# A fused attention and ResMLP kernel: the first pair's lam products and the beta1 of batches 2 and 3 on VectorE, and the second-matmul operand of product 3 cast by every pair

## The chip, the cores and the metric

The kernel runs on one core of a Trainium2 chip. The metric is the device time of one execution in microseconds (us), and the time of a version is the median over its runs. Engines are named as in the profile: PE is TensorE (PEld its weight loads), DVE is VectorE, ACT is ScalarE, POOL is GpSimd, SP is SyncE, which here only issues transfers.

## The reference, cut to what matters

Grouped-query attention (16 query heads, 4 key heads, head size 64, 8 batches of 384 positions) is followed by one ResMLP block on the 1024 channels:

```python
x   = attention(q, k, v)                      # 8 batches of 384 x 1024
a1  = alpha1 * x + beta1
tok = einsum('ts,bsd->btd', w_tok, a1)        # mixes the 384 positions
u   = x + lam * tok
a2  = alpha2 * u + beta2
ch  = maximum(a2 @ w_ch1, 0) @ w_ch2          # 1024 -> 4096 -> 1024
out = u + lam * ch
```

All inputs and the output are float32; the kernel's matmuls take bf16.

## The kernel before

**Pairs and products.** The eight batches are taken in four pairs (pair 0 holds batches 0 and 1, and so on). For a pair, each of the two channel matmuls is done as seven products of half-size blocks in place of eight, from sums and differences of the blocks of both operands. Products are numbered 1 to 7. A pair has a first product stage (`w_ch1`) and a second (`w_ch2`). In the trace the first stage of pair 0 is line 681, its second stage line 752; for pairs 1 to 3 these are lines 831 and 897.

**What runs beside them.** While the second stage of pair i runs, the attention and the token mixing of the two batches of pair i+1 are interleaved with it on every engine: `side(b)` makes the steps of batch b, and a plan (`put(pair, stage, step, function)`) says at which step of the stage each is issued. Each engine works through its instructions in the program's order. For each of the eight column blocks p of a batch, `av_piece` computes attention times v (L295), the reciprocal (L300), x (L303) and alpha1*lam*x; `tok` mixes positions (PE L324), adds (L331) and multiplies by alpha2 (L334); `turn` transposes the result on PE (L398).

**beta1.** For batches 0 to 3 (`fold`) beta1 is not added on DVE. Its effect on tok is an outer product of the row sums of w_tok (R) and of lam*beta1 (H), which PE adds by one more matmul per 128x128 output block (L328); DVE then needs one instruction per block (L309). For batches 4 to 7 DVE does a product (L312) and a sum with h1 = lam*beta1 (L313). H and R lie in the memory of h1, so h1 is loaded (`rows4_on`: two POOL memsets and two small SP transfers; `to_all` L1037; `scale_beta` L1040) only in the first stage of pair 1.

**lam times ch.** Each finished 128x512 piece of ch is multiplied by lam (`scaled`, L790) and added to the output in HBM by an accumulating POOL transfer (`store`, L442). Twelve pieces belong to pair 0; nine of these multiplications are issued in its second stage and three in the first stage of pair 1. For pair 0 they are done on POOL, for later pairs on DVE.

**Operands of the second stage.** Each product has a 2048x512 operand from `w_ch2`, handled as four chunks of 128x2048 bf16 (512 KB). Product 3's operand is the quadrant "22" itself; others are quadrants or differences. In pair 0 the quadrants are read from HBM by POOL transfers that cast float32 to bf16 (L491), DVE forms the differences (`sum_w2`, L499), and `keep_w2` (L494, on SP's queue) writes all 28 chunks to the scratch tensor `w2s` in HBM. Pairs 1 to 3 read them back in the order of `PLACE2` (products 1, 2, 6, 5, 3, 7, 4) by `fetch` (L528, SP's queue) into slots of `w1` or `pad` as PE frees them; product 3 has chunks 16 to 19.

**From pair 0 to pair 1.** At the end of pair 0's second stage DVE forms sums of the turned a2 blocks (`sums_a`, L448 to L450) and of the chunks of w_ch1 (`sum_w1`, L510 and L515). Chunks of w_ch1 are loaded by `load_w1` (POOL, L183) into freed slots; `order1` takes chunk g and chunk g+8 in turn, so the four that open pair 1 are 0, 8, 1, 9. The sum for the next step, `sum_w1(1, 5)`, needs chunk 9. In DVE's order it stands ahead of the sum that makes block 6 of the left operand (L850), which product 3 of the first step needs: that is the tenth of the fourteen matmul groups of a step (`SEQ1`).

Of the kernel before, what the change touches and what calls it, by code (L numbers as in the profile page):

```python
# [13 lines left out]
def kernel(  # L14
# [21 lines left out]
    nc = tc.nc  # L36
# [4 lines left out]
    MUL = mybir.AluOpType.mult  # L41
# [43 lines left out]
    g1, h1, al2, lam_t = (vecs[:, i] for i in range(4))  # L85
# [10 lines left out]
    turn, a2_turn = [0], [0]  # L96
# [21 lines left out]
    SLOTS = 7 * NH // 4  # L118
    w2s = [tc.dram_tile([P, NDT * CW * P], bf, name=f"w2s{i}") for i in range(SLOTS)]
    PLACE2 = {o: i for i, o in enumerate((1, 2, 6, 5, 3, 7, 4))}  # L120

    def by_tok(ap):
        return ap.rearrange("(p st) d -> p st d", st=NST)
# [90 lines left out]
    def side(b):  # L214
        vb = vt[b % 2]
        ess, avs, a1s, a2s, xr = {}, {}, {}, {}, {}
        first, fold = b < 2, b < 4
        kT_, qT_ = kTs.get(b, kT), qTs.get(b, qT)

        def x_of(p):  # L220
# [170 lines left out]
        def by_pe(p):  # L391
            return b in (0, 3) or b % 2 and p >= NP - (4 if first else 3)
# [14 lines left out]
        def put(k, *m):  # L407
            at.setdefault(k, []).append(m)
# [3 lines left out]
        for p in range(NP):  # L412
            put((4, 10, 14, 18, 24, 29, 33, 35)[p], av, p)
            put((8, 15, 17, 22, 27, 32, 36, 38 if b % 2 else 39)[p], tok_flip, p)
            if by_pe(p):
                put(((13, 20, 22, 28, 34, 37, 40, 42) if b == 3 else (0, 0, 0, 0, 0, 36, 39, 41))[p], turn, p)
        return at

    def loads(b):
# [21 lines left out]
    def store(b, ms, dw, o):  # L441
        nc.gpsimd.dma_start(out=by_tok(out[b])[:, ms, dw * 512:(dw + 1) * 512], in_=o, accum_op=ADD)  # L442
# [19 lines left out]
    def spare(i):  # L462
        at = 24 * S + i % 3 * 1024
        return hTf[:, at:at + 1024]

    raw = {}
# [4 lines left out]
    def w2_block(name, c):  # L471
        kh, dw = int(name[0]) - 1, int(name[1]) - 1
        return w2src[:, kh * NH + 4 * c:kh * NH + 4 * c + 4, dw * 512:(dw + 1) * 512]

    def stored(c):
        return w2s[4 * PLACE2[2] + c]

# [13 lines left out]
            nc.gpsimd.dma_start(out=at.rearrange("p (a c) -> p a c", a=4), in_=w2_block(name, c))  # L491

    def keep_w2(o, c):
        nc.sync.dma_start(out=w2s[4 * PLACE2[o] + c], in_=raw[{1: "11", 3: "22", 5: "12", 6: "12", 7: "11", 4: "again"}[o], c][1])  # L494

    def sum_w2(o, c):
        at = lambda name: raw[name, c][1]
        to, x, y = {5: ("12", "12", "11"), 6: ("12", "22", "12"), 7: ("11", "12", "11"), 4: ("again", "again", "12")}[o]
        tt(out=at(to), in0=at(x), in1=at(y), op=SUB)  # L499
        keep_w2(o, c)  # L500
# [17 lines left out]
    w2_slots, w2_at = {}, {}  # L518
# [3 lines left out]
    def place(slot):  # L522
        return ring[:, slot] if slot < RING else pad[:, (slot - RING) * 2048:(slot - RING + 1) * 2048]

    def fetch(i, n):
        w2_slots[i, n] = slot = (pad_free if n in PADDED else w1_free).pop(0)
        w2_at[i, n] = place(slot)
        nc.sync.dma_start(out=w2_at[i, n], in_=w2s[n])  # L528

    def free(slot):  # L530
        (w1_free if slot < RING else pad_free).append(slot)
# [35 lines left out]
    def free_blocks(side, gp):  # L567
        for kind in (side + "1", side + "2"):
            if (kind, gp) in block_slot:
                free(block_slot.pop((kind, gp)))  # L570
# [7 lines left out]
    for i in range(1, NB):  # L578
        heads = [(load_w1, c) for c in order1[:4]] if i + 1 < NB else []
        queue += [(load_w1, c) for c in order1[4:]] + [(fetch, i, n) for n in range(SLOTS - 2)] + heads[:2]  # L580
        queue += [(fetch, i, n) for n in (SLOTS - 2, SLOTS - 1)] + heads[2:]
# [190 lines left out]
    def pair(i):  # L772
        b0 = 2 * i
        lead = i == 0
# [12 lines left out]

        def scaled(o, b, ms, dw, t):
            if o != 2 or not last:
                (nc.gpsimd if lead else nc.vector).tensor_tensor(out=t, in0=t, in1=lam_t[:, dw * 512:(dw + 1) * 512], op=MUL)  # L790
            store(b, ms, dw, t)

        def flush(n=9):
# [18 lines left out]
        if lead:  # L812
            yield from first_product(flush)
            share_banks("sc0", "acc", "sc1", "sc2")
            yield from second_product(pairs["acc"], later, flush, scaled)
            return

        for g in range(NH // 2):
            X, Y, snap = {}, {}, {}
            for k, (o, e) in enumerate(SEQ1):  # L820
                t = 2 * g + e
# [53 lines left out]
        where = {2: (0, 0), 3: (0, 1), 7: (1, 1), 4: (1, 0)}  # L875
        for k, o in enumerate(PLACE2):
            whole = not last and o != 4
            tail = last and o == 4
            for h in range(1 if whole else 2):
                for ms in range(NST - (tail and not h)):  # L880
# [37 lines left out]
                    if (whole or h == 1) and not (last and o == 4):  # L918
                        if o in (1, 6, 5):
                            q = ((1, 6, 5).index(o) * NST + ms) * 512  # L920
                            snap[o, ms] = snaps[:, q:q + 512]
                        else:
                            bb, dw = where[o]
                            t = snap[1, ms] if o == 7 else spare(ms).bitcast(f32)
                        for c0, c1, x in X[ms]:
                            if o == 1:
                                nc.scalar.copy(out=snap[o, ms], in_=x)
                            elif o in (6, 5):
                                tt(out=snap[o, ms], in0=x, in1=snap[1 if last or o == 6 else 6, ms], op=ADD)
                            elif o == 2 and last:  # L930
                                tt(out=t, in0=x, in1=lam_t[:, :512], op=MUL)
                            else:
                                base = {2: 1, 3: 1 if last else 5, 7: 5, 4: 6}[o]
                                tt(out=t[:, c0:c1], in0=x, in1=snap[base, ms][:, c0:c1], op=ADD)
                            if o == 7 and not last:
                                tt(out=snap[6, ms], in0=x, in1=snap[6, ms], op=ADD)
                        if o not in (1, 6, 5):
                            later.append((scaled, o, b0 + bb, ms, dw, t))
# [8 lines left out]
    with tc.manual_schedule(engines=order):  # L947
# [123 lines left out]
        def put(ps, phase, at, *m):  # L1071
            plan.setdefault((ps, phase, at), []).append(m)
# [17 lines left out]
        put(0, 0, 8, rows4_on, (3, 0), (3, 1))  # L1090
        put(0, 0, 30, to_all, 3, 0, 0)
        put(0, 0, 34, to_all, 3, 1, 1)
        put(1, 0, 20, rows4_on, (1, 0), (1, 1))
        put(1, 0, 54, to_all, 1, 0, 0)
        put(1, 0, 68, to_all, 1, 1, 1)
        put(1, 0, 62, scale_beta, 0)
        put(1, 0, 76, scale_beta, 1)
        for c in range(4):
            put(0, 0, (50, 72, 74, 44)[c], load_w2, "11", c)
            put(0, 0, (6, 14, 42, 46)[c], cast_w2, "21", c)  # L1100
            put(0, 1, (41, 43, 45, 47)[c], keep_w2, 1, c)
            put(0, 1, 38 + 2 * c, keep_w2, 3, c)
            put(0, 1, (9, 10, 13, 15)[c], sum_w2, 5, c)
            put(0, 1, (20, 21, 25, 26)[c], sums_first_hid, 2, c)
            put(0, 1, (28, 30, 31, 34)[c], sums_first_hid, 4, c)
            put(0, 1, (37, 40, 41, 43)[c], sum_w2, 6, c)
            put(0, 1, (44, 45, 49, 50)[c], sums_first_hid, 3, c)
            put(0, 1, (51, 54, 57, 58)[c], sum_w2, 7, c)
            put(0, 1, (61, 64, 68, 71)[c], last_w2, c)
        for u, o in ((77, 5), (79, 7), (81, 6)):  # L1110
            put(0, 1, u, sum_w1, 0, o)
        for ps in range(NB - 1):
            c = 2 * ps + 2
            for i in range(9):
                put(ps, 0, (4, 8, 12, 16, 20, 24, 54, 58, 62)[i] if ps == 0 else 4 + 7 * i, load_next, c, 1)
                put(ps, 0, 70 + 3 * i if ps == 0 else 91 + 2 * i, load_next, c + 1, 1)
            put_flips(ps, 0, c, (44, 46, 50, 54, 58) if ps == 0 else range(76, 86, 2))
            put_all(ps, 1, side(c))
            for u, f, h in zip((8, 14, 14, 27, 32, 33) if ps == 0 else (10, 17, 18, 28, 33, 33),
                               (flip_q, flip_k, flip_q, flip_q, flip_k, flip_q), (0, 0, 2, 4, 2, 6)):  # L1120
                put(ps, 1, u, f, c + 1, h, 2)
            put_all(ps, 1, side(c + 1), lambda u: u + 38)
            for j, u in ((0, 77), (2, 80), (3, 83)) if ps == 0 else ((0, 76), (2, 79), (3, 81)):
                put(ps, 1, u, sums_a, j, 1 if j else 2)

        def steps(ps):
            done = [0, 0]
            for second in pair(ps):
                for f, *a in plan.pop((ps, second, done[second]), []):
                    f(*a)  # L1130
                done[second] += 1
                yield
            for key in [k for k in plan if k[0] == ps]:
                for f, *a in plan.pop(key):
                    f(*a)

        first = steps(0)
# [76 lines left out]
```

## Time and profile before

| what | value |
|---|---|
| median of 3 runs | 732.88 us (731.51 to 733.32) |
| the profiled execution's own time | 731.92 us |
| its span in the trace | 729.9 us |
| TensorE clock granted | 1.0 |
| PE busy | 717.4 us |
| DVE busy | 543.9 us |
| POOL busy | 199.2 us |
| DMA queue of POOL (software) | 64.47 MB, 65.4% of 16 engines' span |
| DMA queue of SP (hardware) | 87.42 MB, 42.8% |

The span runs from the first to the last recorded instruction of one execution; 2.0 us of its time lie outside. A busy share is time in which an engine has an instruction in it. "Idle before" gives the idle time of an engine ahead of an instruction and what ended it. The share of a DMA queue is the time of its packets, waiting included, so two queues can add up to more than 100%.

### The profile page before, as it was taken

To read this page: it belongs to the slowest core of one execution; us is meant where nothing else is said; L and a number is where in the kernel's file an instruction comes from. 1 tells how busy PE (TensorE), PEld (TensorE's weight loads), DVE (VectorE), ACT (ScalarE), POOL (GpSimd) and SP (SyncE) were. 2 spreads that over 40 slices of the span, in tenths; PEclk is the share of its full clock that TensorE was granted. 3 is DMA by queue.
4 is the path that set the end of the run, shared out by engine and by line. 5 is a ranking of instruction groups with operands and counts; after the bars stand their busy time and mean duration, and the time that the engine had idled before them with its cause. 6 is when DMAs were issued, how large, how long until landed. Compare 5 with 4: busy or idle time off the path is not lost.

```text
span 729.9 us, 14511 instructions
## 1 busy us (share of the span) xinstructions
PE 717.4 (98%) x5716; PEld 408.7 (56%) x5716; DVE 543.9 (75%) x1009; ACT 373.8 (51%) x566; POOL 199.2 (27%) x242
## 2 busy tenths in 40 slices
PE   8899999999999999999999999999999999999998
PEld 4665555555555666555555566655555566654444
DVE  7888876577888988649678888748868988763354
ACT  7877666544563666643433466663333366650000
POOL 8844233221046551201022344200002222000011
PEclk9999999999999999999999999999999999999999
DMA  9999999999999999969989999998989999937965
GB/s 164 180 239 231 190 195 227 226 242 235 366 312 232 179 182 196 234 221 207 272 193 220 160 162 194 212 227 201 270 233 183 210 126 146 165 123 264 302 174 104
DMA packets 197616, 153.26 MB, mean 210 GB/s; under 512 B 90540, under 2 KB 175892, under 8 KB 197292
## 3 DMA queue, kind: packets, MB, share of 16 engines
q0 software_dynamic: 109872, 64.47, 65.4%
q1 hardware_dynamic: 86988, 87.42, 42.8%
q8 instruction: 44, 0.72, 0.4%
q10 hardware_dynamic: 688, 0.46, 0.2%
q14 instruction: 24, 0.20, 0.1%
HBM read 155.23 MB, written 39.85 MB: 267 GB/s over the span
## 4 chain that ended last, share of the span: by engine, by line
PE 90%; DVE 4%; POOL 2%; DMA 1%; issue 1%; ACT 1%; DVEq 0%; ACTq 0%; POOLq 0%
PE C L897 30%; PE X L831 17%; PE C L752 10%; PE Y L831 9%; PE Z L831 4%; PE sc L260 4%; PE X L681 4%; PE sc L295 3%; PE sc L324 3%; PE Y L681 3%; DMA ops<-obuf 1%; DVE pad L565 1%; PE Z L681 1%; PE tok L324 1%; POOL obuf L334 0%
## 5 line engine op out<-in xcount | busy, mean ns | idle before, releaser
L897 PE MATMUL C<-w,arena 128*128 128x512 bf16 (+2 forms) x744 | 168.3, 372 | 0.0
L269 ACT ACTIVATE es<-sc 128x1024 bf16<-128x1024 f32 x108 | 104.1, 1024 | 116.0 <-PE sc L260 107.6
L897 PEld LDWEIGHTS <-arena 128*128 128x128 bf16 x1040 | 94.8, 98 | 100.5 <-issue 5.1
L442 POOL DMA_DIRECT2D out_dram<-hT x45 | 40.0, 888 | 294.7 <-DVE hT L790 135.9
L836 ACT ACTIVATE hT<-X,bias 128x384 f32<-128x384 f32 x144 | 83.6, 582 | 60.0 <-PE X L831 55.2
L831 PEld LDWEIGHTS <-w 128*128 128x128 bf16 x768 | 75.1, 98 | 50.0
L831 PEld LDWEIGHTS <-pad 128*128 128x128 bf16 x576 | 56.4, 98 | 37.2
L183 POOL DMA_DIRECT2D w<-in_moe_w_ch_dram x48 | 45.4, 1002 | 105.6 <-PE X L831 36.5
L831 PE MATMUL X<-ops,w 128*128 128x384 bf16 x384 | 70.3, 326 | 0.0
L831 PE MATMUL X<-ops,pad 128*128 128x384 bf16 x384 | 70.3, 326 | 0.0
L897 PE MATMUL C<-pad,arena 128*128 128x512 bf16 (+2 forms) x296 | 70.2, 373 | 0.0
L324 PEld LDWEIGHTS <-wtokT 128*128 128x128 bf16 x576 | 39.0, 98 | 16.4 <-issue 3.4
L752 PEld LDWEIGHTS <-arena 128*128 128x128 bf16 x336 | 29.8, 98 | 30.0 <-issue 2.5
L331 DVE TENSOR_TENSOR xr<-sc,xr 128x384 f32<-128x384 f32 x48 | 26.5, 553 | 25.6 <-PE sc L324 14.3
L752 PE MATMUL C<-w,arena 128*128 128x512 bf16 x168 | 41.2, 379 | 0.0
L838 DVE TENSOR_TENSOR arena<-Y,hT 128x384 bf16<-128x384 f32 x48 | 26.5, 556 | 17.7 <-ACT hT L836 16.0
L295 PEld LDWEIGHTS <-es 128*128 128x128 bf16 x864 | 32.8, 97 | 11.3
L831 PE MATMUL Y<-ops,w 128*128 128x384 bf16 x192 | 39.1, 326 | 0.0
L831 PE MATMUL Z<-ops,w 128*128 128x384 bf16 x192 | 39.0, 326 | 0.0
L269 ACT ACTIVATE hT<-sc 128x1024 bf16<-128x1024 f32 x36 | 35.8, 1031 | 4.3 <-PE sc L260 4.0
L260 PE MATMUL sc<-qT,kT 64*128 64x384 bf16 (+2 forms) x504 | 37.2, 271 | 0.5 <-ACT hT L269 0.2
L842 ACT ACTIVATE arena<-X,bias 128x384 bf16<-128x384 f32 x48 | 27.9, 582 | 17.7 <-PE X L831 16.1
(190 smaller groups left out, 1175.1 us busy)
## 6 DMA issues: line engine op xcount, KB each, us to landing
w<-w2s SPq DMA_DIRECT2D x67, 512.0 KB, 5.1
w<-in_moe_w_ch_dram POOLq DMA_DIRECT2D x65, 512.0 KB, 9.8
pad<-w2s SPq DMA_DIRECT2D x25, 512.0 KB, 6.9
out_dram<-hT POOLq DMA_DIRECT2D x45, 256.0 KB, 7.1
out_dram<-xr SPq DMA_DIRECT2D x48, 192.0 KB, 5.3
q_raw<-in_q_dram POOLq DMA_DIRECT2D x28, 192.0 KB, 9.5
w2s<-w SPq DMA_DIRECT2D x10, 512.0 KB, 7.6
arena<-in_moe_w_ch_dram POOLq DMA_DIRECT2D x8, 512.0 KB, 15.9
```

The lines of the kernel that those rows point to most:

```text
L183: nc.gpsimd.dma_start(out=w1[:, w1_slots[c]], in_=w1src[:, :, c * CW * P:(c + 1) * CW * P])
L260: nc.tensor.matmul(out=sc[:, hh, k % 4:k % 4 + n], lhsT=kT_[r, 2 * p // G, BLK[hh][sk], :], rhs=qT_[r, p, st:st + n, :], start=True, stop= ...
L269: nc.scalar.activation(out=e, in_=sc, func=EXP, scale=scale_qk)
L295: nc.tensor.matmul(out=av[:, hh, sq, :], lhsT=ess[k // 4][:, m % 2, k % 4, :], rhs=vb[:, sk, hk, :], start=(sk == 0), stop=(sk == NST - 1))
L324: nc.tensor.matmul(out=ps[:, tt, :], lhsT=wtokT[:, st, tt * P:(tt + 1) * P], rhs=a1s[p][:, st, :], start=(st == 0), stop=(st == NST - 1 an ...
L442: nc.gpsimd.dma_start(out=by_tok(out[b])[:, ms, dw * 512:(dw + 1) * 512], in_=o, accum_op=ADD)
L681: nc.tensor.matmul(out=ps[:, :n], lhsT=tb[G, o][:, dt, e * P:(e + 1) * P], rhs=opb(FIRST1[o], n)[:, dt], start=(o in (1, 2, 7) and dt == 0 ...
L752: nc.tensor.matmul(out=x, lhsT=lead_hid[:, t, FIRST2[o], ms * P:(ms + 1) * P], rhs=rhs[:, t % 4 * 512:(t % 4 + 1) * 512], start=(o in (1, ...
L831: nc.tensor.matmul(out=ps, lhsT=tb[g, o][:, dt, e * P:(e + 1) * P], rhs=opb(LEFT1[o])[:, dt], start=(o in (1, 2, 7) and dt == 0), stop=(dt ...
L836: nc.scalar.activation(out=snap[o, e], in_=ps, func=IDENT, bias=hi if o == 5 else lo)
L842: nc.scalar.activation(out=hid[:, t, 4], in_=ps, func=RELU, bias=hi)
L897: nc.tensor.matmul(out=x, lhsT=hid[:, t, LEFT2[o], ms * P:(ms + 1) * P], rhs=rhs[:, t % 4 * 512 + c0:t % 4 * 512 + c1], start=((not last o ...
```

## The change

Three parts. `fold` now holds for batches 0 and 1 only, so batches 2 and 3 add beta1 on DVE; h1 is loaded in the first stage of pair 0 instead of that of pair 1. The lam multiplication of pair 0 is on DVE like that of the others. Chunks 16 to 19 are no longer written by `keep_w2`; `fetch` reads them from `w_ch2` in each of pairs 1 to 3 by a casting POOL transfer. One PE transpose of batch 3 (block 2) is placed a step later.

```diff
+    RAW2 = {PLACE2[3]: "22"}
-        first, fold = b < 2, b < 4
+        first = fold = b < 2
-                put(((13, 20, 22, 28, 34, 37, 40, 42) if b == 3 else (0, 0, 0, 0, 0, 36, 39, 41))[p], turn, p)
+                put(((13, 20, 23, 28, 34, 37, 40, 42) if b == 3 else (0, 0, 0, 0, 0, 36, 39, 41))[p], turn, p)
     def keep_w2(o, c):
-        nc.sync.dma_start(out=w2s[4 * PLACE2[o] + c], in_=raw[{1: "11", 3: "22", 5: "12", 6: "12", 7: "11", 4: "again"}[o], c][1])
+        nc.sync.dma_start(out=w2s[4 * PLACE2[o] + c], in_=raw[{1: "11", 5: "12", 6: "12", 7: "11", 4: "again"}[o], c][1])
     def fetch(i, n):
-        nc.sync.dma_start(out=w2_at[i, n], in_=w2s[n])
+        if n // 4 in RAW2:
+            nc.gpsimd.dma_start(out=w2_at[i, n].rearrange("p (a c) -> p a c", a=4), in_=w2_block(RAW2[n // 4], n % 4))
+        else:
+            nc.sync.dma_start(out=w2_at[i, n], in_=w2s[n])
         def scaled(o, b, ms, dw, t):
-                (nc.gpsimd if lead else nc.vector).tensor_tensor(out=t, in0=t, in1=lam_t[:, dw * 512:(dw + 1) * 512], op=MUL)
+                nc.vector.tensor_tensor(out=t, in0=t, in1=lam_t[:, dw * 512:(dw + 1) * 512], op=MUL)
-        put(1, 0, 20, rows4_on, (1, 0), (1, 1))
-        put(1, 0, 54, to_all, 1, 0, 0)
-        put(1, 0, 68, to_all, 1, 1, 1)
-        put(1, 0, 62, scale_beta, 0)
-        put(1, 0, 76, scale_beta, 1)
+        put(0, 0, 40, rows4_on, (1, 0), (1, 1))
+        for i in range(2):
+            put(0, 0, 54 + 10 * i, to_all, 1, i, i)
+            put(0, 0, 59 + 10 * i, scale_beta, i)
-            put(0, 1, 38 + 2 * c, keep_w2, 3, c)
```

## The prediction

> **What bounds the kernel now.** I read the page's engine shares first, then the busy time by stretches of 20 us, then the chain of waits from 215 us on, and last the groups of instructions and the timeline around the places that stand out.
>
> ```profile
> span 729.9 us, 14511 instructions
> PE 717.4 (98%) x5716; PEld 408.7 (56%) x5716; DVE 543.9 (75%) x1009; ACT 373.8 (51%) x566; POOL 199.2 (27%) x242
> ...
> 200.00:220.00 20.00, 19.41 (x194) 10.97 (x193) 16.81 (x24) 12.64 (x19) 8.04 (x8) 1.00 1.19 309
> 220.00:240.00 20.00, 18.81 (x141) 10.53 (x138) 16.51 (x28) 8.84 (x17) 10.48 (x11) 1.00 1.18 227
> 240.00:260.00 20.00, 20.00 (x125) 12.04 (x124) 19.15 (x31) 13.21 (x23) 12.06 (x14) 1.00 1.38 178
> ```
>
> The columns after the stretch are its length, then PE, PEld, DVE, ACT and POOL busy, the clock, the DMA share and GB/s. PE sets the end: from 240 to 720 us every stretch has it 20.00 of 20. Its idle 12.5 us (729.9 - 717.4) are the head (some 7 us to 120 us), the tail (3.6) and 1.8 in 200 to 240 us, the end of pair 0's second stage. So this change can gain in two ways, PE work removed and those 1.8 us; what it adds elsewhere costs only where it makes PE wait.
>
> ```profile
> 218.18 0.06 PE sc L328
> ...
> 220.87 2.02 DVE w L499
> ...
> 223.62 1.09 DVE a L309
> 224.71 0.04 issue
> 224.76 0.34 PE sc L324 x3
> ```
>
> This is the chain (start, length, what). A beta1 matmul holds it for 0.06 us, and at 224.76 PE waits for DVE's L309.
>
> ```profile
> L309 DVE TENSOR_TENSOR a<-xr,vecs 128x384 bf16<-128x384 f32 x16 | 11.8, 736 | 0.6
> L312 DVE TENSOR_TENSOR a1f<-xr,vecs 128x384 f32<-128x384 f32 x32 | 17.9, 558 | 1.1
> L313 DVE TENSOR_TENSOR a<-a1f,vecs 128x384 bf16<-128x384 f32 x32 | 17.8, 557 | 1.1
> L790 DVE TENSOR_TENSOR hT<-hT,vecs 128x512 f32<-128x512 f32 x30 | 20.6, 686 | 0.4
> L790 POOL TENSOR_TENSOR hT<-hT,vecs 128x512 f32<-128x512 f32 x12 | 18.6, 1552 | 17.6 <-ACT hT L764 17.6
> ...
> 225.19 1.56 POOL L790 TENSOR_TENSOR hT<-hT,vecs 128x512 f32<-128x512 f32 x1
> 225.44 1.74 DVE L309 TENSOR_TENSOR a<-xr,vecs 128x384 bf16<-128x384 f32 x1
> ```
>
> The same DVE product takes 0.56 us undisturbed (L312) and 1.74 beside a POOL product: the two block each other, and L309's mean of 736 ns is 16 x 0.18 = 2.9 us of such blocking.
>
> **The change part by part.** *PE work removed.* 16 blocks lose three L328 matmuls each, 48 in all. In the chain a mixing step takes 3 x (0.17 + 0.06) us with them and 0.50 without (batches 4 and 5), so 0.17 per block and 16 x 0.17 = 2.7 us. All of it lies where PE is the chain, between 138 and 228 us.
>
> *DVE in pair 0's second stage.* Added: 16 x 0.56 (a product becomes a product and a sum) = 8.9 us and nine lam products x 0.69 = 6.2 us. Returned: the blocking, 2.9 us on L309 and some 2.6 on others (L334 at 212.75 took 1.77 for 0.56, L499 at 220.87 2.02 for 1.22, L334 at 149.16 1.05 for 0.56). Net +9.6 us. Between 142 and 229 us DVE has about 14 us of idle time, most of it before 193. There the extra work is covered: at 156.5, 163, 169, 178.7 and 189 DVE waited 1.0 to 1.9 us for PE, more than the 0.6 to 1.2 that one block gains. Without that cover it would be up to 9.6 us. The cover ends at 212 us, so I walk the rest in the order of the new program.
>
> *The walk.* I use starts on DVE, one to the next, since instructions overlap by some 0.08 us: L303 and L312 0.59, L313, L309 and L334 0.47, L331 0.58, L300 0.22, lam 0.61, L499 1.14, L767 0.60. DVE waits last for ACT's copy of C that ended at 214.7; thirteen mixing steps lie ahead of it, so it comes 13 x 0.17 = 2.2 earlier, at 212.5. From there DVE has, without a pause, two L767 (1.2), three sets of L300, L303, product and sum (3 x 1.87 = 5.6), six lam products (3.7), two L499 (2.3), three pairs of L331 and L334 (3.2), one L515 (0.6) and the first three `sums_a` (1.5): 18.1 us, and the sixth lam product ends at 230.6. In the walk the wait of 0.95 us at 224.76 remains: the sum ends at 222.1 where PE is ready at 221.1. PE reaches the end of the stage at 231.7 instead of 234.54, 2.8 earlier.
>
> *What is late next.* DVE's `sums_a` end near 233.7 and PE wants block 0 at 233.0: some 0.4 us. More decides the load of chunk 9. On POOL's queue it stands behind the six stores, and each store now waits for DVE's lam product instead of POOL's own; so do the loads and k, q and v transfers behind it. Before, the last store was issued at 227.05 and chunk 9 at 232.10, when PE freed its slot:
>
> ```profile
> 232.10 0.92 POOL L183 DMA_DIRECT2D w<-in_moe_w_ch_dram  x1 [4.17 <-PE sc L398]
> ...
> 238.07 0.69 DVE L515 TENSOR_TENSOR pad<-w 128x1024 bf16<-128x1024 bf16 x1 [2.92 <-DMA w<-in_moe_w_ch_dram]
> ...
> 238.68 0.95 DVE L850 TENSOR_TENSOR ops<-ops 128x1536 bf16<-128x1536 bf16 x1
> ```
>
> DVE stood 2.92 us for that chunk, and L850, which PE's group at 240.39 needs, came right behind it: 0.76 us in hand. Now the sixth store is issued at 230.7 and chunk 9 at 231.6, only 0.5 earlier than before, while PE has come 2.8 earlier. With the 5.9 us to landing that it had, it lands at 237.6; POOL's software queue carries the late store ahead of it (the last six stores took 11.6 falling to 7.5 us to land, a queue working off a backlog), so I take 238.0, between that and a delay of one store's spacing (1.7 us). Then L515 (0.61) and L850 (0.95) end at 239.6, and PE's group starts there, not at 240.39: **0.8 us of the 2.7 are left**, the rest goes into a wait of about 1.5 us before that group and 0.4 before block 0.
>
> A fixed-cost rule speaks for more. The Trainium skill, page "DMA: Bandwidth & Descriptors", section "Anatomy of one DMA", gives a software transfer about 2.0 us plus its bytes at 436 GB/s; my estimate from it is 4.4 us for the 1 MB read here, and the sum would be that of the first rival. The trace has 5.6 to 13.7 us for these loads, and I go by the trace.
>
> *Pair 1's first stage.* Three lam products move to DVE (2.1 us), the h1 work leaves it (two L1037 of 0.72, two L1040 of 0.68: 2.8 us), and the blocking at 244.57 (L861 1.90 for 0.36) and 246.57 (L863 1.43 for 0.56) goes. DVE gains; nothing for PE, which has no wait there. *First stage of pair 0.* The same 2.8 us and two memsets (0.6 each, POOL idle) arrive; DVE waited 1.8 to 2.2 us for PE once in each group of 9.4 us there, which covers about 1.2 a group. Bounds 0 to 0.6 us, I take 0. The later transpose costs nothing: PE does it anyway.
>
> *Product 3's chunks.* Four writes of 512 KB leave SP's queue in the stretch where it is busiest (0.4 to 1.6 us of issue each). Twelve SP reads (landing 3.1 to 8.9 us) become POOL casts, issue 0.75 us each. In pair 1 SP issued chunks 16 to 19 at 339.5, 346.9, 350.0 and 353.3; PE uses them first at 365.2, 366.6, 367.4 and 369.1, so 16 to 26 us in hand. POOL is idle from 339.6 to 371.9, and the stores ahead of them in its order are out by 338.75. Such casts took 5.8 to 22.7 us, the long ones six in a row; these come 3 to 7 us apart, and I take 13: hidden. Pair 2 is the same to 1 us; in pair 3 the hand is 16 to 20 us. Bounds: 0, and 22.7 - 15.8 = 6.9 us for each of pairs 1 to 3.
>
> *Sum.* Span 729.9 - 2.7 + 1.9 = 729.1; the profiled execution 731.92 becomes 731.1. It lay 0.96 below the median of the runs, so against 732.88 the forecast is **732.1 us**.
>
> **Rivals.** *The full PE gain.* If chunk 9 lands by 236.4, L850 is in time and only 0.4 is lost: 732.88 - 2.4 = 730.5. For it: stores landed in 4.1 us at other places, SP's writes of product 3 no longer share the engines. Against: no load landed in under 5.6. *Slower: POOL's queue behind DVE.* If the late store and three loads run into a queue still full, chunk 9 takes what the loads at 251 to 272 us took (8.5 to 13.7 us, behind stores). With 10.6 us it lands at 242.2, L850 ends at 243.8, 3.4 after the group's old start: 736.3. It decides above a landing of 7.2 us, where the gain is gone. For it: the median of these loads, 9.4; against: that neither the loads of k, q and v nor spills crowd this moment. *Casts not hidden.* At the upper bound 3 x 6.9 = 21 us, 754; with a landing of 17.8 us, 2 each, 739. *DVE binds the whole second stage* or the change does less on PE than it says: the built programs show 48 matmuls and weight loads fewer, and DVE would need its 9.6 us uncovered: 732.9 - 2.7 + 5 = 735 at half.
>
> **How the numbers follow.** Forecast 0.45, full gain 0.22, POOL's queue 0.23, casts 0.06, DVE 0.04. A change under 0.3% (2.2 us) can't be told from none here. Faster beyond it is the full gain and the forecast's edge (0.24), slower most of the last three (0.30), the rest 0.46. The forecast's own range is 731.6 to 734.1 (landing 5.9 to 8.4); the whole range takes in the full gain and the queue's typical case: 729.9 to 736.6.
>
> **What would show it.** L328 with 48 matmuls fewer and L309 or its successors at 0.56 us; no POOL product at L790; the idle time of DVE's L515 before L850, and PE waiting for L850 in its first step of pair 1; chunk 9 issued right behind a store near 231.6. PE waits at line 897 in pairs 1 to 3 would prove the casts wrong; a stage boundary 2.8 us earlier with no wait behind it the first rival right.

## The result and the profile after

The changed kernel took 736.91 us (median of 20 runs), the kernel before 732.6 us beside it: a ratio of 1.0068 (95% interval 1.005 to 1.0086). That is 4.3 us slower; 732.1 was forecast, 0.8 us faster than the kernel before. The ratio leaves out the executions that were counted as slow, the medians hold all. The profiled execution took 736.13 us with a span of 734.4, 4.5 more than the span before. Line numbers have moved by one to four: L790 is now L794, L831 L835, L850 L854, L515 L516, L183 L184, L442 L443.

First the page's head (shares, the PE row and the clock row in 40 slices of 18 us) and the busy time by stretches (length, PE, PEld, DVE, ACT, POOL, clock, DMA share, GB/s), of the changed kernel:

```profile
span 734.4 us, 14411 instructions
PE 718.7 (98%) x5668; PEld 406.4 (55%) x5668; DVE 551.1 (75%) x1037; ACT 373.6 (51%) x566; POOL 190.4 (26%) x242
...
PE   8899999999998899999999999999999999999998
...
PEclk9999999999999899999999999999999999999999
```

```profile
200.00:220.00 20.00, 19.76 (x205) 10.94 (x204) 18.93 (x31) 14.66 (x21) 3.53 (x4) 1.00 1.09 288
220.00:240.00 20.00, 16.68 (x107) 8.63 (x103) 13.51 (x28) 6.98 (x13) 6.84 (x8) 1.00 1.06 185
240.00:260.00 20.00, 18.34 (x97) 10.37 (x98) 15.42 (x28) 10.36 (x17) 7.49 (x9) 0.83 1.10 148
```

PE has 48 matmuls fewer and yet is busy 1.3 us longer; in 240 to 260 us it got through 97 recorded matmuls (125 before) at a granted clock of 0.83 (1.00 before). Two things are new: a gap around 240 us, and slow products behind it.

The groups that the change was to touch did what it says:

```profile
L794 DVE TENSOR_TENSOR hT<-hT,vecs 128x512 f32<-128x512 f32 x42 | 28.8, 686 | 0.7 <-ACT hT L768 0.4
L313 DVE TENSOR_TENSOR a1f<-xr,vecs 128x384 f32<-128x384 f32 x48 | 26.8, 558 | 1.7
L314 DVE TENSOR_TENSOR a<-a1f,vecs 128x384 bf16<-128x384 f32 x48 | 26.8, 558 | 1.7
```

All 42 lam products are on DVE at 0.69 us and no product with beta1 takes longer than undisturbed. PE began the first stage of pair 1 at 231.08 us, 3.3 earlier than before (234.38). Then the gain was lost. The waits of PE and of DVE between 200 and 260 us (total, times, longest), POOL's timeline, and the chain of waits (start, length, what), all of the changed kernel:

```profile
PE X L835 <- DVE ops L854: 3.8, 1, 3.8
PE sc L325 <- DVE a L314: 0.7, 1, 0.7
...
DVE pad L516 <- DMA w<-in_moe_w_ch_dram: 6.2, 1, 6.2
```

```profile
226.69 0.85 POOL L443 DMA_DIRECT2D out_dram<-hT  x1 [0.57 <-DVE hT L794]
230.48 0.84 POOL L443 DMA_DIRECT2D out_dram<-hT  x1 [2.94 <-DVE hT L794]
231.05 2.98 POOL L184 DMA_DIRECT2D w<-in_moe_w_ch_dram  x3
```

```profile
231.05 8.97 DMA w<-in_moe_w_ch_dram
...
240.04 0.70 DVE pad L516
...
240.78 0.83 DVE ops L854
...
241.66 2.74 PE X L835 x8
244.40 1.28 PE Z L835 x4
245.68 2.04 PE Y L835 x8
247.72 1.30 PE X L835 x8
```

Read upwards from 241.66: PE's group waits for L854, L854 stands on DVE behind L516, L516 waits for chunk 9, and chunk 9 is the first of three loads that POOL could issue only after the sixth store, which had waited 2.94 us for its lam product on DVE. Read downwards: after 3.8 us of idle time the same twenty products that take 1.30 + 0.65 + 1.30 = 3.25 us take 6.06. The chain before had this last group at 243.64; now it is at 247.72. So 1.27 us is a later start (241.66 against 240.39) and 2.81 us are slow products: 4.08 of the 4.5. The last 0.4 was not followed.

### The profile page after: what moved, and what is told of

Its sections match the earlier page's. It is cut to its first block, busy times and chain, and to the rows that moved or that the text cites. A ratio compares the mean times of both kernels' runs of the same rounds, so it can differ in the third digit from the quotient of the medians.

```text
span 734.4 us, 14411 instructions
## 1 busy us (share of the span) xinstructions
PE 718.7 (98%) x5668; PEld 406.4 (55%) x5668; DVE 551.1 (75%) x1037; ACT 373.6 (51%) x566; POOL 190.4 (26%) x242
## 4 chain that ended last, share of the span: by engine, by line
PE 88%; DVE 6%; POOL 3%; issue 1%; DMA 1%; ACT 1%; DVEq 0%; POOLq 0%; ACTq 0%
PE C L901 30%; PE X L835 17%; PE Y L835 8%; PE C L756 8%; PE sc L261 4%; PE Z L835 4%; PE sc L296 3%; PE X L685 3%; PE sc L325 3%; PE Y L685 2%; DMA w<-in_moe_w_ch_dram 1%; PE E L617 1%; PE tok L325 1%; PE av L296 1%; DVE pad L569 1%
## 5 line engine op out<-in xcount | busy, mean ns | idle before, releaser
L443 POOL DMA_DIRECT2D out_dram<-hT x45 | 39.5, 879 | 311.9 <-DVE hT L794 184.6
L835 PEld LDWEIGHTS <-w 128*128 128x128 bf16 x768 | 75.6, 99 | 55.3 <-DVE ops L854 4.2
L835 PEld LDWEIGHTS <-pad 128*128 128x128 bf16 x576 | 56.7, 98 | 38.7 <-issue 2.0
L835 PE MATMUL X<-ops,w 128*128 128x384 bf16 x384 | 71.5, 330 | 3.8 <-DVE ops L854 3.8
L184 POOL DMA_DIRECT2D w<-in_moe_w_ch_dram x48 | 46.6, 1058 | 95.8 <-PE X L835 30.2
L835 PE MATMUL X<-ops,pad 128*128 128x384 bf16 x384 | 70.2, 326 | 0.4 <-ACT hT L840 0.4
L325 PEld LDWEIGHTS <-wtokT 128*128 128x128 bf16 x576 | 37.4, 98 | 16.5 <-issue 3.3
L835 PE MATMUL Z<-ops,w 128*128 128x384 bf16 x192 | 39.7, 330 | 0.0
L835 PE MATMUL Y<-ops,w 128*128 128x384 bf16 x192 | 39.2, 326 | 0.0
L842 DVE TENSOR_TENSOR arena<-Y,hT 128x384 bf16<-128x384 f32 x48 | 26.3, 556 | 16.3 <-ACT hT L840 14.7
```

The lines of the kernel that those rows point to most:

```text
L184: nc.gpsimd.dma_start(out=w1[:, w1_slots[c]], in_=w1src[:, :, c * CW * P:(c + 1) * CW * P])
L325: nc.tensor.matmul(out=ps[:, tt, :], lhsT=wtokT[:, st, tt * P:(tt + 1) * P], rhs=a1s[p][:, st, :], start=(st == 0), stop=(st == NST - 1 an ...
L835: nc.tensor.matmul(out=ps, lhsT=tb[g, o][:, dt, e * P:(e + 1) * P], rhs=opb(LEFT1[o])[:, dt], start=(o in (1, 2, 7) and dt == 0), stop=(dt ...
```

## The experiments

Each was run beside the kernel before on the same chip. "Wait" is PE's longest wait in the first stage of pair 1, "chunk 9" the time from its issue on POOL to DVE's start on it, both from the one profiled execution ("hidden" where DVE came to it later than it landed). The ratio is not the quotient of the two medians beside it: for `a_no_raw` these give 1.0057, for `a_fold_back` 1.0041. Some executions also lost time to a transfer that came late elsewhere, as two profiles below show, so the place of a loss is read from the traces and the ratio only says whether the time agrees.

| run | median us (before beside it) | ratio, 95% interval | wait us | chunk 9 us |
|---|---|---|---|---|
| after_again | 737.03 (733.38) | 1.0056, 1.0029 to 1.0083 | 4.0 | 8.92 |
| a_no_raw | 737.89 (733.68) | 1.0018, 0.9982 to 1.0054 | 4.4 | 9.25 |
| a_fold_back | 736.72 (733.68) | 1.0020, 0.9989 to 1.0051 | 3.8 | 9.28 |
| b_lam_dve | 736.02 (733.38) | 1.0037, 1.0019 to 1.0055 | 3.6 | 9.11 |
| a_lam_pool | 734.26 (733.68) | 1.0009, 0.9972 to 1.0046 | none | 5.82 |
| a_op6_early | 734.84 (733.68) | 0.9994, 0.9953 to 1.0035 | 3.6 | 10.25 |
| a_sums_late | 732.20 (733.38) | 1.0007, 0.9978 to 1.0037 | 0.7 | 8.72 |
| a_sums_late_no_raw | 733.91 (733.97) | 0.9999, 0.9972 to 1.0026 | 0.5 | 8.79 |
| b_sums_late | 732.29 (733.97) | 0.9984, 0.9954 to 1.0015 | none | hidden |
| a_store_early | 732.65 (733.97) | 0.9975, 0.9950 to 1.0001 | 0.7 | 6.99 |
| a_store_early_2 | 731.25 (733.36) | 0.9982, 0.9955 to 1.0008 | 0.2 | 5.71 |
| a_store_early_no_raw | 733.00 (733.36) | 0.9995, 0.9964 to 1.0026 | 0.8 | 7.52 |
| a_store_early_sums_late | 732.72 (733.97) | 0.9980, 0.9948 to 1.0013 | 0.9 | hidden |
| b_lam_store_early | 734.10 (733.36) | 0.9992, 0.9960 to 1.0024 | 1.7 | 8.41 |
| b_hold3 | 738.66 (733.36) | 1.0081, 1.0054 to 1.0109 | 2.7 | 6.38 |
| b_hold6 | 753.49 (733.38) | 1.0281, 1.0257 to 1.0304 | 5.4 | 6.08 |

**Which part loses?** The changed kernel again, for the comparison on the same chip:

> The changed kernel itself, beside the others on the same chip: 1.0068 of before, with PE's wait of 3.8 us for L854 and a granted clock near 0.83 in 240 to 260 us.

Three runs undo one part of the change each, one makes one part alone. Product 3 stored again (`a_no_raw`):

```diff
-    RAW2 = {PLACE2[3]: "22"}
...
+            put(0, 1, 38 + 2 * c, keep_w2, 3, c)
```

> The changed kernel with product 3's W2 chunks stored in bf16 again and read by SP's queue. Late chunk: nothing of this is near 230 us; the time stays within 1 us of 736.9, with the wait for L854 and the lower clock. Rival, casts: 730 to 732.5, with the loss gone.

The wait stayed (4.4 us, clock 0.91 in 240 to 260 us), chunk 9 took 9.25 us and the median lay 4.2 us above the one beside it. The ratio, 1.0018 (0.9982 to 1.0054), can't be told from none, so it is the trace that says it: the wait and the slow products are there without the casts.

beta1 back on PE (`a_fold_back`; the later transpose and the loading of h1 go back with the line shown):

```diff
-        first = fold = b < 2
+        first, fold = b < 2, b < 4
```

> The changed kernel with batches 2 and 3 taking beta1 by TensorE again (48 matmuls back, 16 sums off DVE, the later transpose and the beta1 rows as before). Late chunk: the six lam products stay on DVE, so the sixth store is out near 231 and chunk 9 lands near 240, while PE comes 2 to 2.7 us later; PE's wait for L854 is 1 to 2 us, too short for the clock to drop: 733 to 735. Rival, DVE: the sums are what hurts, 732.6 or less. Rival, casts: 736.9 + 2.7 = 739.6.

The wait was not 1 to 2 us but 3.8 again, with a clock of 0.83; the time, 1.0020 (0.9989 to 1.0051), decides nothing here. I had thought that DVE is bound by its own work, so that a later PE would meet the same DVE. But with the mixing matmuls back DVE waits for PE and moves with it: PE's stage began at 234.26, the sixth store came at 232.62, chunk 9 was taken at 242.47. From the sixth store to the start of the stage there were 1.6 us here and 0.6 in the changed kernel, and the store still stood in front of the load.

lam alone on DVE, the rest as before (`b_lam_dve`):

```diff
-                (nc.gpsimd if lead else nc.vector).tensor_tensor(out=t, in0=t, in1=lam_t[:, dw * 512:(dw + 1) * 512], op=MUL)
+                nc.vector.tensor_tensor(out=t, in0=t, in1=lam_t[:, dw * 512:(dw + 1) * 512], op=MUL)
```

> The kernel before with one part alone: the first pair's lam products on VectorE. Late chunk: the sixth store waits for a lam product behind DVE's sums and chunk 9 is issued right behind it; PE waits some 3 to 4 us for L850 and the clock drops; without the PE work removed: before + 3.5 to 6.5, ratio 1.005 to 1.009. Rival, only the three parts together do it: ratio 0.998 to 1.002.

It loses by itself: 1.0037, a little under the forecast, with a wait of 3.6 us for L850 and chunk 9 taking 9.11 us. The moved lam products are the part that makes the loss.

The opposite edit in the changed kernel, lam back on POOL (`a_lam_pool`):

> The changed kernel with the first pair's lam products back on POOL. Late chunk: the stores ahead of chunk 9 wait for POOL's own products again and are out by some 227 us, chunk 9 is issued when PE frees its slot near 230 and lands by 237; PE's wait for L854 is below 1.5 us and the clock stays at 1.00: 732.6 - 2.7 + 0.5 to 1.5 of blocking between POOL's and DVE's products = 730.4 to 731.5. Rival, casts: 736.9 stays. Rival, DVE: the three sums stay on DVE and the blocking comes back on top, 735 or more.

Half of this held. The sixth store was out at 226.72, chunk 9 took 5.82 us, and nothing waited for L854. But the time was 734.26, not 731, since a wait grew elsewhere. PE's waits between 200 and 260 us, DVE's timeline and two rows of PE's, of that run:

```profile
PE sc L325 <- DVE a L314: 4.2, 2, 3.1
```

```profile
214.26 2.45 DVE L313 TENSOR_TENSOR a1f<-xr,vecs 128x384 f32<-128x384 f32 x1
216.74 2.46 DVE L314 TENSOR_TENSOR a<-a1f,vecs 128x384 bf16<-128x384 f32 x1
```

```profile
219.25 1.14 PE L325 MATMUL sc<-a,wtokT 128*128 128x128 bf16 x9 [3.12 <-DVE a L314]
...
227.49 0.68 PE L325 MATMUL sc<-a,wtokT 128*128 128x128 bf16 x9 [1.12 <-DVE a L314]
```

DVE's two instructions of 0.56 us took 2.45 each while POOL's products ran, and PE waits 3.1 us for the second. The nine products behind that wait took 1.14 us in place of 0.68, at a granted clock of 0.50 (220 to 222 us); with those after them some 1.6 us went there on top of the wait. In this run lam on POOL beside beta1 on DVE pays that blocking, so the two parts belong together. The Trainium skill, page "SBUF — State Buffer", section "Who interferes with whom", has it that a DVE instruction with both inputs in SBUF contends with a GpSimd instruction that reads SBUF. The trace agrees, and has the size: 4.4 times the undisturbed duration.

**Who stands behind the late chunk?** One line moved in the changed kernel (`a_op6_early`):

```diff
-                if k == 3 and g == 0:
-                    tt(out=opb(6), in0=opb(4), in1=opb(5), op=SUB)
                 if k == 2 and g == 0:
                     sum_w1(0, 4)
+                    tt(out=opb(6), in0=opb(4), in1=opb(5), op=SUB)
```

> The changed kernel with one line moved: the sum opb(6) (L854) stands ahead of the sum that takes chunk 9, no longer behind it on DVE. Late chunk (the theory: chunk 9 is loaded behind six stores that wait for DVE's lam products, DVE stands for it in order, L854 comes late, PE idles 3.8 us, and the clock granted after that idle time costs some 2.8 us more): no PE wait for L854, granted clock 1.00 from 240 to 260 us, chunk 9 itself as late as before (issued near 231, landed near 240), and the 2.7 us of PE work come through: 732.6 - 2.7 + 0.4 = 730.3, bounds 729.5 to 731.5. Rival, casts (product 3's casts cost the time): nothing changes, 736.9. Rival, DVE (its added work makes PE late all through the stage): at most the 1.6 us of L516 and L854 are saved, 735 or more.

The wait for L854 went, and a wait of 3.6 us for L842 came, the next instruction on DVE behind the chunk; the time, 0.9994 (0.9953 to 1.0035), can't be told from that of before. Waits and chain of that run:

```profile
PE Y L835 <- DVE arena L842: 3.6, 1, 3.6
```

```profile
243.47 2.72 PE Y L835 x8
246.19 1.40 PE X L835 x8
```

So the expectation was wrong in that it freed only one of the instructions behind the wait. The mending has to take the wait itself out of the way (`a_sums_late`):

```diff
-                if k in (2, 5, 8, 11) and g + 1 < NH // 2:
-                    sum_w1(g + 1, {2: 5, 5: 7, 8: 6, 11: 4}[k])
+                at = {8: 5, 9: 7, 10: 6, 12: 4} if g == 0 else {2: 5, 5: 7, 8: 6, 11: 4}
+                if k in at and g + 1 < NH // 2:
+                    sum_w1(g + 1, at[k])
```

> The changed kernel; in the first group of pair 1's first stage alone, DVE's four sums that take chunk 9 stand at steps 8, 9, 10 and 12 instead of 2, 5, 8 and 11. Chunk 9 is loaded as late as in the changed kernel. Late chunk, with DVE standing for it in order (the theory): DVE does L854, L842 and L844 first, PE has nothing of DVE's to wait for before block 1, which it wants near 242.4, some 1 us after the sums end; no PE wait over 1 us, clock 1.00, and the time is that of before - 2.7 + 0.7 (the wait at L325) = before - 2.0, ratio 0.997. Rival, the loss is in the landing itself (queue and engines loaded, not DVE's order): the wait moves to block 1's product and stays 2 us or more with the clock drop, ratio 1.003 or more. Rival, casts or DVE's work: ratio 1.006 as before.

Chunk 9 was as late (issued at 231.03, taken at 239.75), yet PE waited no longer than 0.7 us here and the clock stayed at 1.00 from 200 to 500 us: the loss needs DVE's order, not the late load alone. The time is less clear. The median is 732.2, 1.2 below before, but the ratio 1.0007 (0.9978 to 1.0037; the changed kernel on the same chip had 1.0056) has an interval that also holds the rival's lower edge, 1.003. The profiled execution lost time at a place of its own, in the second stage of a later pair:

```profile
PE C L902 <- DMA w<-w2s: 3.9, 2, 2.1
```

Two reads from `w2s` came late there, at 576 and 579 us; no other execution profiled here shows them late. The waits, 1.8 and 2.1 us with 1.0 us of products between them, were followed by some 3.0 us of slow products at a clock of 0.50. Without these 6.9 us the span of 735.6 would be an estimated 728.7, 1.2 below before. The casts of that stage had been issued by 521.6 us, 42 us ahead of the late read; what made it late was not followed. The control on the kernel before:

> A control: the kernel before with the sums of chunk 9 late in the first group. L850 had 0.76 us in hand there, so nothing waits for it: theory, ratio 0.998 to 1.002. Rival, the later sums are a gain of their own, whatever the change does: ratio 0.997 or less.

0.9984 (0.9954 to 1.0015): no gain that can be told from none, as the theory has it.

> The changed kernel with the sums of chunk 9 late in the first group and product 3's chunks stored in bf16 again. If product 3's casts cost nothing, as forecast: the same as with the casts, 731 to 732.5, ratio 0.997 to 1.000, no PE wait at L902's line in pairs 1 to 3 with or without. Rival, the casts load POOL's queue and make the slow executions of the changed kernel (739 to 746): they come less often here, and the median is 1 us or more lower than with the casts.

0.9999 against 1.0007 with the casts: no difference that these runs can show.

**What makes the chunk late?** The six lam products and stores are handed out closer together (`a_store_early`, and a second time as `a_store_early_2`), so that the sixth stands on DVE ahead of the next stage's first sums:

```diff
-                    if t % 8 == 3 and later and (later[0][1] == 1 or k > 16 and later[0][1] != 4):
+                    if (t % 8 == 3 or k > 16) and later and (later[0][1] == 1 or k > 16 and later[0][1] != 4):
```

> The changed kernel with the six lam products and their stores handed out at every fourth chunk step of the last turns, not every second, so that the sixth lam product stands on DVE ahead of the first sums of the next stage. DVE does the same work and still stands for chunk 9 in order. Late chunk, by the sixth store ahead of it in POOL's queue (the theory): the sixth store is issued near 227.5 instead of 230.5, chunk 9 when PE frees its slot near 229.5, it lands by 235.5 to 237.5, PE's wait for L854 is 0 to 2 us, the clock stays at 1.00: 730 to 732.5, before - 1 to - 3, ratio 0.996 to 0.999. Rival, chunk 9 is slow because its transfer shares the engines with what else runs then: it takes 8 to 9 us from its issue all the same and lands near 238.5; the wait is 2 to 3 us, ratio 1.000 to 1.002. Rival, DVE's work: PE's waits at L325 grow instead, ratio 1.005.

> The changed kernel with the stores handed out early, a second time beside the two above: theory, before - 1 to - 3, ratio 0.996 to 0.999, below before and below the changed kernel (1.0068 and 1.0056). Rival, it only takes back the loss: 0.999 to 1.001.

POOL's timeline in `a_store_early`, with DVE's line for chunk 9, and PE's waits behind it:

```profile
226.60 0.84 POOL L443 DMA_DIRECT2D out_dram<-hT  x1 [1.12 <-DVE hT L794]
230.36 0.92 POOL L184 DMA_DIRECT2D w<-in_moe_w_ch_dram  x1 [2.92 <-PE sc L399]
232.59 1.78 POOL L184 DMA_DIRECT2D w<-in_moe_w_ch_dram  x2 [1.31 <-PE C L756]
```

```profile
237.35 0.69 DVE L516 TENSOR_TENSOR pad<-w 128x1024 bf16<-128x1024 bf16 x1 [3.12 <-DMA w<-in_moe_w_ch_dram]
```

```profile
PE X L835 <- DVE ops L854: 0.3, 1, 0.3
```

The store is out 3.9 us earlier, the load now waits for PE to free its slot (the bracket names PE, not DVE), takes 6.99 us and 5.71 in the second run, and the wait for L854 falls from 3.8 us to 0.3 and to none. The second run's profile has a span of 728.5 at clock 1.00, 1.4 below that of before. Price: PE's waits at L325 grew from 0.7 to 1.9 us. The medians are 1.3 and 2.1 us below before; each interval reaches just over 1. Taken together as independent, the two ratios give an estimate of 0.9979, from 0.9960 to 0.9997 (their mean, and their half-widths in quadrature over two). So this version probably beats the kernel before by some 1.5 us; against the changed kernel (1.0068 and 1.0056) the gain is clear.

> The changed kernel with the stores handed out early, and product 3's chunks stored in bf16 again. The casts as forecast (hidden): the same as a_store_early, ratio 0.996 to 0.999. Rival, the casts cost: 1 us or more lower than a_store_early, which runs beside it.

> Both mendings in the changed kernel: the stores handed out early, and the sums of chunk 9 late in the first group. Theory: no PE wait behind 231 us, all of the PE work's gain is left, before - 2.0 to - 3.0, ratio 0.996 to 0.997, and both kernels are beaten. Rival: no more than with one of them, ratio 0.999 or more.

Without the casts the ratio is 0.9995 (0.9964 to 1.0026): no cost of the casts shows. With both mendings it is 0.998 (0.9948 to 1.0013): the second adds nothing to the first. Its profiled span of 738.2 has its loss in the head, in the first attention scores:

```profile
PE sc L261 <- DMA arena<-q_raw: 6.5, 1, 6.5
```

And the same mending with lam as the only part of the change:

> The kernel before with the lam products on VectorE, and the six products and stores handed out early as in a_store_early; beta1 and product 3 as before. Theory: the loss of 2.7 us or more that this part alone made goes, chunk 9 is issued when PE frees its slot, PE's wait for L850 is under 1 us, clock 1.00; ratio 0.998 to 1.001 of before, since no PE work is removed. Rival, lam on VectorE costs by DVE's own time: 1.003 or more stays.

0.9992 (0.996 to 1.0024) where lam alone had 1.0037: the loss goes, as expected. The wait was 1.7 us, more than the bound of 1, because chunk 9 took 8.4 us although the sixth store was 4.0 us ahead of it (231.31 and 235.31). So the place of the store is not all of the landing. In the eight traces with the load issued 0.57 us behind the store (all rows of the table from 8.72 to 10.25 us, and the changed kernel's 8.99) it took 8.7 to 10.3 us; in those with 3.8 us or more between them (before with 5.97, and the rest of the table) it took 5.7 to 7.5 seven times and 8.4 once. In the first group the three loads also left POOL at once, in the second the second came 2.2 us behind the first. Which of the two, the store ahead or the loads behind, costs the 2 to 3 us was not told apart.

**What does the idle time itself cost?** In the kernel before, L850 done seven times over (`b_hold6`) and four times over (`b_hold3`):

```diff
+                    for _ in range(7):
-                    tt(out=opb(6), in0=opb(4), in1=opb(5), op=SUB)
+                        tt(out=opb(6), in0=opb(4), in1=opb(5), op=SUB)
```

> The kernel before with L850 done seven times over, so that PE's group waits for DVE while no transfer is later: 6 x 0.87 - 0.76 = 4.5 us of PE idle time. Clock theory: the granted clock falls to about half for some 4 us after it, the next groups take twice as long, and the time is before + 4.5 + 2 to 3.5 = 6.5 to 8. Rival (the slow products after the wait came from the queues or the buffers): clock 1.00, before + 4.5.

> The kernel before with L850 done four times over in each of pairs 1 to 3. With seven times over, PE waited 5.4 us in pair 1 and 4.2 in pairs 2 and 3; three sums of 0.97 us fewer leave some 2.5, 1.3 and 1.3, 5.1 in all. Clock theory (what is charged behind the wait depends on its length, and sets in above some 3 us): the clock stays at 1.00 and the time is before + 5.1, bounds 4 to 6. Rival, every wait costs about 2 us more behind it: before + 11.

The first expectation was written for one wait; the edit acts in pairs 1, 2 and 3, with 13.8 us of waits in all. The time grew by 20.1, so 6.3 us, 2.1 for each wait, come on top. PE's timeline (start, length, the idle time before it in brackets) in the third of these pairs, and then that of `b_hold3` in the first and the third:

```profile
605.66 2.74 PE L831 MATMUL X<-ops,w 128*128 128x384 bf16 x8 [4.25 <-DVE ops L851]
608.20 1.48 PE L831 MATMUL Z<-ops,w 128*128 128x384 bf16 x4
609.48 2.41 PE L831 MATMUL Y<-ops,pad 128*128 128x384 bf16 x8
611.72 1.46 PE L831 MATMUL X<-ops,w 128*128 128x384 bf16 x8
```

```profile
244.75 2.29 PE L831 MATMUL X<-ops,w 128*128 128x384 bf16 x8 [2.68 <-DVE ops L851]
...
249.69 1.46 PE L831 MATMUL X<-ops,w 128*128 128x384 bf16 x8
...
595.72 1.48 PE L831 MATMUL X<-ops,w 128*128 128x384 bf16 x8 [1.28 <-DVE ops L851]
...
598.99 1.46 PE L831 MATMUL X<-ops,w 128*128 128x384 bf16 x8
```

From start to start the twenty products take 3.27 us behind a wait of 1.28 (598.99 - 595.72), 4.94 behind 2.68 and 6.06 behind 4.25. Chunk 9 took 6.1 and 6.4 us in these two kernels, hardly more than before (5.97), so the slow products are PE's own, at the lower clock. `b_hold3` had waits of 5.2 us and grew by 5.3 in the median (4.0 to 8.0 by the ratio's interval), far from its rival's 11. In its trace the two waits of 1.3 us cost their own length; the one of 2.68 us cost 1.7 more, below the 3 us that I had set.

## Why the prediction was wrong

**The step that failed** is the landing of chunk 9, "I take 238.0", and with it the price of the wait that a late landing makes. The walk to it held: DVE's sixth lam product ended at 230.18 (walked: 230.6), chunk 9 was issued at 231.05 (231.6) and PE began the next stage 3.3 us earlier than before (2.8 walked). The landing was sized from the row of before, 5.9 us, plus a little for the store ahead; it took 8.97, to 240.0. With that, L854 ended at 241.6 instead of 239.6, past PE's old start of 240.39. These 2.0 us alone would have stayed at the edge of the forecast's own range: its upper end, 734.1, is a landing at 240.0. The rival "POOL's queue behind DVE" named this place and this chain; its median of 9.4 us for the loads of before was nearer to what came than the one row of 5.9 that the forecast went by.

**The term that was missing** is the price of the wait. Forecast and rival both counted a wait at its own length. It took 2.8 us more in slow products, over half of the loss, and these take the sum from 734.1 to 736.9. That the rival's 736.3 lies near the measured time is luck: its landing at 242.2 was 2.2 us too late, while this term was left out.

**What held.** PE's 48 matmuls went and the stage began 3.3 us earlier (2.8 forecast). The blocking between POOL's and DVE's products went with lam's move, and `a_lam_pool` shows what it would have cost: 2.45 us for 0.56. The sum waited for by L325 costs PE 0.7 us (0.95 forecast). The casts of product 3 are hidden: from 260 to 700 us the changed kernel's profile lists no wait of PE at all, and kernels with and without them differ by less than the runs can tell. DVE did not bind the whole second stage.

**The full PE gain** could be had in part: `a_store_early_2` reaches a span 1.4 us below before, against the 2.4 of that rival. Its waits at L325 are 1.2 us longer than the changed kernel's, about as much as the rest; that they are the whole of it was not shown.

## What to carry to other kernels

When a product moves from one engine to another, follow what its result releases: here the store behind it, the queue that the store sits in, and the load behind the store. A wait stands in the order of its engine, so moving one waiting instruction shows only the next one; move the wait, or what is late. And count a PE wait of some 2.7 us or more, or two shorter ones close together, at its length plus 1.4 to 3 us of slow products behind it.

## What the hardware showed that was not expected

A PE wait of 2.7 to 5.4 us was followed in every trace read by products at half speed for a time, and so were the two waits of 1.8 and 2.1 us in `a_sums_late`: 1.4 to 3.0 us lost, not in proportion to the wait (5.35 us cost 1.4, 3.8 cost 2.8). Single waits of 1.3 and 1.7 us cost nothing more. The half speed does not begin at a fixed point either: in the timelines the first eight products took 2.29 us behind 2.68 us, 1.80 behind 4.36 us (`a_no_raw`) and 2.74 behind 3.8 us, where full speed is 1.46.

The granted clock in short stretches shows why. The changed kernel, with the columns of the stretches shown first (the clock is the third from the end):

```profile
240.00:241.00 1.00, 0.00 (x0) 0.00 (x0) 0.96 (x2) 0.00 (x0) 0.00 (x0) 0.61 1.43 193
241.00:242.00 1.00, 0.34 (x2) 0.18 (x3) 1.00 (x2) 0.00 (x0) 0.00 (x0) 0.50 1.47 200
...
247.00:248.00 1.00, 1.00 (x7) 0.59 (x6) 0.79 (x2) 0.00 (x0) 1.00 (x2) 0.97 1.06 110
```

The clock fell to 0.50 at 240.2, while PE still waited, and came back at 247.1. PE resumed at 241.66, so 5.4 us of work ran at half speed, which is 2.7 us lost (2.81 in the chain). Read in the same way in stretches of 0.1 us, the clock stood at 0.50 for 3.41 us in six of the twelve such places that were read and for 6.83 us, twice that, in the other six; it fell between 2.1 us before PE resumed and 1.0 us after. In `b_hold6` the three falls (246.16, 423.65 and 604.56 us) lie 52 and 53 times 3.413 us apart, so they follow a grid of their own and not the wait. In the 3.41 us ahead of a fall PE had been idle for 2.0 to 3.4 us in all; a stretch of the grid with 1.95 us (`a_no_raw`, from 237.44) brought no fall. So in these traces it is the idle time within one stretch that decides, some 2 us of it, and the place of the wait on the grid sets the price.

The Trainium skill, page "TensorE: Matmul & The Clock Gate", section "Part 1: The HAM clock gate", says that PE's clock is halved after an idle window of about 3.4 us and comes back after about as long of activity, by windows that run freely. The traces agree on the half clock (0.50), on the length (3.41 us) and on the free run (the grid of `b_hold6`). An estimate from the page's window, one to two of them at half speed, is 1.7 to 3.4 us lost; 1.4 to 3.0 were measured, the least where PE still waited in a part of the window. They differ on the threshold: one wait of 2.68 us was enough, and so were 2.0 us of idle time within a window (`a_fold_back`).
